# Two tiles centred without their standard deviation, and seven q tiles parked as fp32 copies, in a fused linear-attention and SwiGLU kernel

## The chip, the cores and the metric

One core of one Trainium2 chip. The metric is the device time of the kernel in microseconds (us); lower is better. The engines are TensorE (PE, with its weight loads shown as PEld), VectorE (DVE), ScalarE (ACT), GpSimd (POOL) and SyncE (SP, which here only issues DMAs).

## The reference

The input `x` is 2048 x 512 in bf16. It is normalised once, and both branches read the normalised `xn`:

```python
def _A_ref(x, wqkv, wo):
    H = 32; Dh = D // H                       # D = 512, Dh = 16
    qkv = (x @ wqkv) split into q, k, v by head
    phi = lambda t: jnp.where(t > 0, t + 1, jnp.exp(t)) + 1e-6
    pq, pk = phi(q), phi(k)
    kv = jnp.einsum("bhsd,bhse->bhde", pk, v)
    z = jnp.einsum("bhsd->bhd", pk)
    num = jnp.einsum("bhqd,bhde->bhqe", pq, kv)
    den = jnp.einsum("bhqd,bhd->bhq", pq, z)[..., None] + 1e-6
    return (num / den) @ wo

def _B_ref(x, w_gate, w_up, w_down):          # F = 1792
    return (silu(x @ w_gate) * (x @ w_up)) @ w_down

xn = _layernorm(x)                            # (x - mean) / sqrt(var + 1e-5)
return x + _A_ref(xn, A_wqkv, A_wo) + _B_ref(xn, B_w_gate, B_w_up, B_w_down)
```

## The kernel before

**Order.** The kernel is written as one list of operations for all engines. `K.add` notes for each operation its engine, what it reads and what it writes, and derives the semaphore waits; each engine then runs its own operations strictly in the order of the list. There is no scheduler behind it: the order is written out by hand as a string of steps, `run("S0 R0 S1 L0 ...")`, a letter for the step and a number for the tile of 128 rows. There are 16 tiles.

**Stage 1, the string.** For tile t:
- `S` takes the row statistics on DVE (L228, L231); `R` computes `ln(var + eps)` and then `exp(-0.5 ...)` = 1/std on ACT (L235, L237).
- The tile is normalised to `xn` by one of three steps: `L` on DVE (L241), `N` and `A` on POOL and ACT (L246, L251), or `P` on POOL (L256, L259).
- `xn` is transposed to `xnT`: tiles 0, 1 and 2 on PE (`T`, L269), with the PSUM result copied out by ACT (`E`, L276) or DVE (`V`, L278); the other 13 by a DMA transpose that SP issues (`D`, L284).
- `k` and `q` are the projections (L297), each four matmuls of 512 columns into one PSUM bank. The banks 4 to 7 are used in a ring: a projection takes the bank of the fourth one before it, and waits until that bank's readers are through.
- The feature map is computed in three steps. ACT takes the exp of the bank (`x`, `y`, L305), POOL limits it to 1 (`m`, `n`, L309), and DVE adds `max(bank, 1e-6)` and writes `pk` or `pq` (`s`, `u`, L316).
- `G` accumulates `xn^T pk` over the tiles in the banks 0 to 3 (L321).

Ahead of the string PE runs ten matmuls on a constant, `keep_busy(NWARM, 512)` (L218), and within it two of 256 columns (`F2`).

**Stage 2, the feed-forward loop.** 56 steps `gu(j)` each compute one gate and one up block of 128 x 512 (L384), ACT takes the silu (L392) and DVE multiplies (`hop`, L397) into `hT[C % 2, fc]`. C counts the four chunks of four tiles. In the first steps the sums that the attention branch still needs are put in between: the copies of G (`gt_evac`), the sum of `pk` over the tiles (`z_add`, L334, tiles 0 to 9 on POOL and 10 to 15 on DVE), and the matmul that spreads z. Later steps carry the denominators (`pz_mul`, `divide`). From the second chunk on, `otile` computes the output tiles (L463, L467) and writes them out.

**DMAs.** SP issues the x tiles and half of the qkv weights first, then the transposes `D` in the order of the string, and behind the last of them the weights of stage 2 (`fload`, `dload`); ACT issues three loads at the start.

Of the kernel before, what the change touches and what calls it, by code (L numbers as in the profile page):

```python
# [9 lines left out]
P = 128  # L10
# [10 lines left out]
HPG = P // DH  # L21
NH = D // DH

NWARM = 10
NFILL = 3
O_SLOT = {4: 0, 7: 1, 10: 2, 13: 3}
PZ_AT = {9 + 11 * t // 4: t for t in range(16)}
DIV_AT = {j + 1: t for j, t in PZ_AT.items()}
# [79 lines left out]
def bass_parallel_sum__linear_attn_block__swiglu_ffn__prompt_kernel(nc, A_x, A_wqkv, A_wo, B_x, B_w_gate, B_w_up, B_w_down, out):  # L108
# [5 lines left out]
    with contextlib.ExitStack() as es:  # L114
# [4 lines left out]

        x_sb = sb("x_sb", [P, NT, D], bf)  # L120
        xn = sb("xn", [P, NT, D], bf)
        xnT = sb("xnT", [P, NDC, S], bf)
        wqkv = sb("wqkv", [P, NDC, 3 * D], bf)
        wo = sb("wo", [P, NG, D], bf)
# [24 lines left out]
        lnv = sb("lnv", [P, NT], f32)  # L149
        rstd = sb("rstd", [P, NT], f32)  # L150
        nm = sb("nm", [P, NT], f32)
        banks = [E(nc.psum_tensor("pb%d" % i, [P, 512], f32)) for i in range(8)]

        def B(i):
            return ("bank", i)
# [27 lines left out]


        K.add("act", lambda e: e.preload_act_table_set("natural_log_exp_and_others"))
        for h, eng in ((0, "sp"), (1, "act")):
            load(eng, ("x", 0, h), x_sb[:, 0, h * 256:h * 256 + 256], xin[0:P, h * 256:h * 256 + 256])
        xload("sp", 1)
        wload("act", 1, 0, 2)
        wload("sp", 1, 1, 2)  # L190
        xload("act", 2)
        wload("act", 0, 0, 2)
        xload("sp", 3)
        wload("sp", 0, 1, 2)
        for t in range(4, 16):
            xload("sp", t)

# [24 lines left out]


        def xk(t):
            return [("x", t)] if t else [("x", 0, 0), ("x", 0, 1)]

        def bn1(t):
            K.add("dve", lambda e: e.bn_stats(stats[:, t, :], x_sb[:, t, :]), r=xk(t), w=[("st", t)])  # L228
# [4 lines left out]
        def rs(t):  # L233
            sl = slice(t, t + 1)
            K.add("act", lambda e: e.activation(lnv[:, sl], mv[:, t, 1:2], ACT.Ln, bias=eps5[:, :], scale=1.0),  # L235
                  r=[("mv", t), ("eps5",)], w=[("lnv", t)])
            K.add("act", lambda e: e.activation(rstd[:, sl], lnv[:, sl], ACT.Exp, scale=-0.5),  # L237
                  r=[("lnv", t)], w=[("rs", t)])

        def lna_dve(t):  # L240
            K.add("dve", lambda e: e.tensor_scalar(  # L241
# [24 lines left out]

        def transp(t, b, lo=0, hi=NDC):
            tb = tview(b, hi - lo)
            K.add("pe", [(lambda e, c=c: e.transpose(tb[:, c - lo, :], xn[:, t, c * P:(c + 1) * P], ident[:, :]))  # L269
                         for c in range(lo, hi)], r=[("xn", t), ("ident",)], w=[B(b)])  # L270

        def evac(t, b, eng="act", lo=0, hi=NDC):
            src = tview(b, hi - lo)
            dst = xnT[:, lo:hi, t * P:(t + 1) * P]
            if eng == "act":
                K.add("act", lambda e: e.activation(dst, src, ACT.Copy), r=[B(b)], w=[("xnT", t, lo)])  # L276
            else:
                K.add("dve", lambda e: e.tensor_copy(dst, src), r=[B(b)], w=[("xnT", t, lo)])  # L278

        def xkeys(t):  # L280
            return [("xnT", t, 0), ("xnT", t, 2)] if t == 0 else [("xnT", t, 0)]

        def dmat(t):
            K.add("sp", lambda e: e.dma_start_transpose(out=xnT[:, :, t * P:(t + 1) * P], in_=xn[:, t, :]),  # L284
                  r=[("xn", t)], w=[("xnT", t, 0)], dma=True)


        ring = [0]
# [3 lines left out]
            ring[0] += 1  # L292
            return 4 + (ring[0] - 1) % 4

        def proj(col, i, t):
            b = nextbank()
            K.add("pe", [(lambda e, c=c: e.matmul(  # L297
                banks[b][:, :], xnT[:, c, t * P:(t + 1) * P], wqkv[:, c, col:col + D],
                start=(c == 0), stop=(c == NDC - 1))) for c in range(NDC)],
                r=xkeys(t) + [("wqkv", i, 0), ("wqkv", i, 1)], w=[B(b)])  # L300
            at[i, t] = b

        def phi_exp(i, t):
            b = at[i, t]
            K.add("act", lambda e: e.activation(ef[:, b - 4, :], banks[b][:, :], ACT.Exp), r=[B(b)], w=[("ef", b - 4)])  # L305

        def phi_min(i, t):
            buf, bkey = ef[:, at[i, t] - 4, :], ("ef", at[i, t] - 4)
            K.add("pool", lambda e: e.tensor_scalar(  # L309
                out=buf, in0=buf, scalar1=1.0 + 1e-6, scalar2=0.0, op0=ALU.min, op1=ALU.max),  # L310
                r=[bkey], w=[bkey])

        def phi_sum(i, t):
            b = at[i, t]
            dst, dkey = ((pk[:, t, :], ("pk", t)) if i else (pq[:, t, :], ("pq", t)))
            K.add("dve", lambda e: e.scalar_tensor_tensor(  # L316
                out=dst, in0=banks[b][:, :], scalar=1e-6, in1=ef[:, b - 4, :], op0=ALU.max, op1=ALU.add),
                r=[B(b), ("ef", b - 4)], w=[dkey])

        def gacc(t):  # L320
            K.add("pe", [(lambda e, c=c: e.matmul(  # L321
                banks[c][:, :], xn[:, t, c * P:(c + 1) * P], pk[:, t, :],
                start=(t == 0), stop=(t == NT - 1))) for c in range(NDC)],
                r=[("xn", t), ("pk", t)], w=[B(c) for c in range(NDC)])


        NZP = 10
# [1 line left out]
        def z_add(half, i):  # L329
            acc, key = zacc[:, half, :], ("zacc", half)  # L330
            t = NZP * half + i
            first, fkey = (pk[:, t - 1, :], ("pk", t - 1)) if i == 1 else (acc, key)
            K.add("dve" if half else "pool",
                  lambda e: e.tensor_tensor(out=acc, in0=first, in1=pk[:, t, :], op=ALU.add),  # L334
                  r=[fkey, ("pk", t)], w=[key])

        def stat(t):
            bn1(t)
            bn2(t)

        steps = {
            "S": stat, "R": rs, "L": lna_dve, "P": lna_pool, "N": nmr, "A": lna_act, "T": lambda t: transp(t, t % 4),
            "E": lambda t: evac(t, t % 4), "V": lambda t: evac(t, t % 4, "dve"), "D": dmat,
            "k": lambda t: proj(D, 1, t), "x": lambda t: phi_exp(1, t), "m": lambda t: phi_min(1, t), "s": lambda t: phi_sum(1, t),
            "q": lambda t: proj(0, 0, t), "y": lambda t: phi_exp(0, t), "n": lambda t: phi_min(0, t), "u": lambda t: phi_sum(0, t), "G": gacc,
            "F": lambda t: keep_busy(t, 256)}

        def run(text):
            for w in text.split():
                steps[w[0]](int(w[1:]))  # L350

        run("""
            S0 R0 S1 L0 R1 L1 S2 T0 E0 F2 T1 V1 R2 L2 k0 k1 x0 m0 S3 T2 S4 x1 m1 E2 R4 s0 q1 R3 L4 k2 x2 N3 A3
            q2 s1 m2 y1 S5 R5 G0 D4 S6 s2 n1 G1 q0 y2 G2 D3 u1 R6 q4 N5 A5 S8 y0 k3 n2 N6 A6 u2 k4 y4 x3 n0 x4
            n4 m3 u0 m4 S13 D5 q3 R8 u4 s3 P8 D6 S7 k5 y3 R13 D8 n3 G3 s4 x5 k6 R7 S9 R9 N7 q6 G4 m5 A7 u3 s5
            S12 x6 q5 G5 N9 m6 S10 A9 y6 s6 y5 q8 R10 D7 k8 N13 n6 R12 u6 y8 G6 n5 x8 D9 u5 A13 k7 x7 S15 S11 k9
            P10 n8 u8 x9 R11 m8 D10 s8 m7 q9 m9 R15 P15 s7 y9 q7 G7 k10 D13 n9 L11 L12 s9 y7 q10 D11 G8 y10 n7
            n10 S14 G9 R14 x10 u7 u9 u10 k11 m10 N14 x11 s10 D15 q13 y13 A14 D12 m11 n13 s11 q11 y11 k12 D14 u13
            x12 m12 k13 k15 n11 x15 m15 u11 G10 x13 m13 s12 G11 q15 q14 y15 n15 s13 s15 k14 x14 m14 y14 q12 s14
            G12 y12 n12 n14 u15 G13 G14 u14 u12 G15  # L360
        """)
        fload("sp", "wg", wg, B_w_gate, 0)
        fload("sp", "wu", wu, B_w_up, 0)
# [31 lines left out]
        def hop(j):  # L395
            C, fc = j // NFC, j % NFC
            K.add("dve", lambda e: e.tensor_tensor(  # L397
                out=hT[:, C % 2, fc, :], in0=banks[gb(j) + 1][:, :], in1=sil[:, j % 2, :], op=ALU.mult),
                r=[B(gb(j) + 1), ("sil", j % 2)], w=[("hT", C % 2, fc)])


        def gt_evac(c, eng):
# [34 lines left out]
        def divide(t):  # L437
            i = t % 2
            K.add("dve", lambda e: e.tensor_reduce(  # L439
                out=den[:, i, :], in_=heads(pz[:, i, :]), axis=mybir.AxisListType.X, op=ALU.add),  # L440
                r=[("pz", i)], w=[("den", i)])
            K.add("dve", lambda e: e.tensor_scalar(
                out=den[:, i, :], in0=den[:, i, :], scalar1=1e-6, scalar2=None, op0=ALU.add),
                r=[("den", i)], w=[("den", i)])
            K.add("dve", lambda e: e.reciprocal(rden[:, i, :], den[:, i, :]), r=[("den", i)], w=[("rden", i)])
            K.add("dve", lambda e: e.tensor_tensor(  # L446
                out=heads(pq[:, t, :]), in0=heads(pq[:, t, :]),
                in1=rden[:, i, :][:, :, None].broadcast_to([P, NH, DH]), op=ALU.mult),
                r=[("pq", t), ("rden", i)], w=[("pq", t)])
            K.add("sp", lambda e: e.dma_start_transpose(  # L450
                out=pk[:, t, :].rearrange("p (g s) -> p g s", g=NG), in_=pq[:, t, :]),
                r=[("pq", t)], w=[("pk", t)], dma=True)
# [113 lines left out]
```

## Time and profile before

| | |
|---|---|
| median of 6 runs | 213.4 us (213.19 to 213.69) |
| profiled execution, its own time | 213.16 us |
| its span | 211.5 us |
| granted TensorE clock | 1.00 |
| PE busy | 207.9 us, 98% of the span |
| DVE, ACT, POOL busy | 125.3, 69.8 and 55.6 us |
| first projection matmul starts | 6.54 us |
| first gate matmul starts | 48.48 us |
| issue of the first gate weights | 39.15 us |

The profile shows one execution, recorded by the hardware. Busy time is summed by engine; a matmul's recorded length includes its way through the array, so that matmuls overlap, and a PE that is called busy need not run at its peak. The times within the trace start with the span. Groups of instructions are named by the line of the kernel, the engine, and the tiles written and read.

### The profile page before, as it was taken

The numbers are of one execution on the slowest core, as the hardware profiler recorded it, in microseconds if no ns is written. First come the engines' busy times: TensorE is split into PE (matmuls) and PEld (weight loads), VectorE is DVE, ScalarE is ACT, GpSimd is POOL, SyncE is SP. The second block draws the span as 40 slices with busy tenths as digits, with TensorE's granted clock in tenths as the row PEclk, the third lists the DMA queues.
The fourth block names the chain that finished last, engine by engine and source line by source line (L and its number), as shares of the span: only waits on it lengthen the run. The fifth ranks groups of instructions, "written<-read, shape, count | busy, mean of one in ns | idle before, by whom it ended". The sixth has DMA issues, their size and how long they took to land.

```text
span 211.5 us, 2659 instructions
## 1 busy us (share of the span) xinstructions
PE 207.9 (98%) x991; PEld 95.9 (45%) x991; DVE 125.3 (59%) x217; ACT 69.8 (33%) x138; POOL 55.6 (26%) x81
## 2 busy tenths in 40 slices
PE   7999999999999999999999999999999999999996
PEld 2444444444544444444444444444444444444455
DVE  3899985546874788664654765573649453532121
ACT  3797974546364333122131313021123122130000
POOL 3267665559923222220210220120204000000000
PEclk9999999999999999999999999999999999999999
DMA  5942423499910021103101011101011101100101
GB/s 180 356 114 48 77 58 68 105 382 371 357 52 0 4 49 25 50 0 53 25 25 40 9 29 50 25 25 50 17 35 25 50 16 39 25 25 9 40 25 53
DMA packets 26765, 15.78 MB, mean 75 GB/s; under 512 B 16512, under 2 KB 26752, under 8 KB 26752
## 3 DMA queue, kind: packets, MB, share of 16 engines
q1 hardware_dynamic: 25920, 14.88, 25.3%
q10 hardware_dynamic: 832, 0.72, 1.0%
q8 instruction: 8, 0.13, 0.3%
q14 instruction: 5, 0.04, 0.1%
HBM read 9.70 MB, written 2.10 MB: 56 GB/s over the span
## 4 chain that ended last, share of the span: by engine, by line
PE 96%; DMA 1%; DVE 1%; ACT 1%; SPq 0%; issue 0%
PE pb L384 46%; PE pb L467 23%; PE pb L297 13%; PE pb L463 7%; PE pb L321 7%; DMA x_sb<-in_A_x_dram 1%; PE pb L409 0%; PE pb L457 0%; DVE stats L228 0%; ACT ef L305 0%; ACT xnT L276 0%; DVE out_sb L473 0%; DVE xn L241 0%; SPq L159 0%; PE pb L269 0%
## 5 line engine op out<-in xcount | busy, mean ns | idle before, releaser
L392 ACT ACTIVATE sil<-pb 128x512 bf16<-128x512 f32 x56 | 33.3, 597 | 101.2 <-PE pb L384 98.8
L397 DVE TENSOR_TENSOR hT<-pb,sil 128x512 bf16<-128x512 f32 x56 | 38.0, 687 | 36.2 <-PE pb L384 33.4
L384 PE MATMUL pb<-xnT,wg 128*128 128x512 bf16 x224 | 57.8, 379 | 0.0
L384 PE MATMUL pb<-xnT,wu 128*128 128x512 bf16 x224 | 57.8, 379 | 0.0
L467 PE MATMUL pb<-wd,hT 128*128 128x512 bf16 (+1 forms) x238 | 51.2, 366 | 0.0
L434 POOL TENSOR_TENSOR pz<-pq,zbc 128x512 f32<-128x512 bf16 x16 | 18.6, 1162 | 86.0 <-DVE den L439 78.5
L467 PEld LDWEIGHTS pb<-wd,hT 128*128 128x128 bf16 x238 | 23.3, 98 | 25.1
L384 PEld LDWEIGHTS pb<-xnT,wu 128*128 128x128 bf16 x224 | 21.9, 98 | 26.0
L384 PEld LDWEIGHTS pb<-xnT,wg 128*128 128x128 bf16 x224 | 21.9, 98 | 25.9
L473 DVE TENSOR_TENSOR out_sb<-pb,x_sb 128x512 bf16<-128x512 f32 (+1 forms) x17 | 11.2, 660 | 33.5 <-PE pb L467 33.5
L297 PE MATMUL pb<-wqkv,xnT 128*128 128x512 bf16 x128 | 29.6, 379 | 0.1
L309 POOL TENSOR_SCALAR ef<-ef 128x512 bf16<-128x512 bf16 x32 | 19.4, 612 | 19.1 <-ACT ef L305 18.9
L305 ACT ACTIVATE ef<-pb 128x512 bf16<-128x512 f32 x32 | 18.3, 591 | 9.4 <-PE pb L297 9.3
L297 PEld LDWEIGHTS pb<-wqkv,xnT 128*128 128x128 bf16 x128 | 12.3, 98 | 15.1 <-ACT xnT L276 0.6
L446 DVE TENSOR_TENSOR pq<-pq,rden 128x512 bf16<-128x512 bf16 x16 | 17.5, 1094 | 0.6
L463 PE MATMUL pb<-M,pk 128*128 128x512 bf16 (+1 forms) x68 | 16.6, 366 | 0.0
L321 PE MATMUL pb<-pk,xn 128*128 128x512 bf16 x64 | 15.4, 379 | 0.0
L316 DVE SCALAR_TENSOR_TENSOR pk<-pb,ef 128x512 bf16<-128x512 f32 x16 | 10.8, 679 | 4.9 <-POOL ef L309 4.9
L316 DVE SCALAR_TENSOR_TENSOR pq<-pb,ef 128x512 bf16<-128x512 f32 x16 | 10.7, 682 | 3.9 <-POOL ef L309 3.9
L228 DVE BATCH_NORM_STATS2 stats<-x_sb 128x6 f32<-128x512 bf16 x16 | 10.9, 679 | 3.3 <-DMA x_sb<-in_A_x_dram 3.3
L439 DVE TENSOR_REDUCE den<-pz 128x32 f32<-128x512 f32 x16 | 10.8, 675 | 0.0
L334 POOL TENSOR_TENSOR zacc<-zacc,pk 128x512 f32<-128x512 f32 x8 | 10.3, 1292 | 0.6
(46 smaller groups left out, 76.8 us busy)
## 6 DMA issues: line engine op xcount, KB each, us to landing
out_dram<-out_sb SPq DMA_DIRECT2D x15, 128.0 KB, 1.7
x_sb<-in_A_x_dram SPq DMA_DIRECT2D x14, 128.0 KB, 4.3
wg<-in_B_w_gate_dram SPq DMA_DIRECT2D x2, 896.0 KB, 7.9
wu<-in_B_w_up_dram SPq DMA_DIRECT2D x2, 896.0 KB, 9.9
wd<-in_B_w_down_dram SPq DMA_DIRECT2D x2, 896.0 KB, 13.8
wqkv<-in_A_wqkv_dram ACTq DMA_DIRECT2D x2, 256.0 KB, 4.2
wqkv<-in_A_wqkv_dram SPq DMA_DIRECT2D x2, 256.0 KB, 4.7
wqkv<-in_A_wqkv_dram SPq DMA_DIRECT2D x1, 512.0 KB, 8.0
```

The source lines that it names most:

```text
L297: K.add("pe", [(lambda e, c=c: e.matmul(banks[b][:, :], xnT[:, c, t * P:(t + 1) * P], wqkv[:, c, col:col + D], start=(c == 0), stop=(c == ...
L305: K.add("act", lambda e: e.activation(ef[:, b - 4, :], banks[b][:, :], ACT.Exp), r=[B(b)], w=[("ef", b - 4)])
L309: K.add("pool", lambda e: e.tensor_scalar(out=buf, in0=buf, scalar1=1.0 + 1e-6, scalar2=0.0, op0=ALU.min, op1=ALU.max), r=[bkey], w=[bkey])
L316: K.add("dve", lambda e: e.scalar_tensor_tensor(out=dst, in0=banks[b][:, :], scalar=1e-6, in1=ef[:, b - 4, :], op0=ALU.max, op1=ALU.add), ...
L321: K.add("pe", [(lambda e, c=c: e.matmul(banks[c][:, :], xn[:, t, c * P:(c + 1) * P], pk[:, t, :], start=(t == 0), stop=(t == NT - 1))) for ...
L384: fns.append(lambda e, c=c, b=b, w_=w_: e.matmul(banks[b][:, :], w_[:, c, fc * P:(fc + 1) * P], xnT[:, c, C * 512:(C + 1) * 512], start=(c ...
L392: K.add("act", lambda e: e.activation(sil[:, j % 2, :], banks[gb(j)][:, :], ACT.Silu), r=[B(gb(j))], w=[("sil", j % 2)])
L397: K.add("dve", lambda e: e.tensor_tensor(out=hT[:, C % 2, fc, :], in0=banks[gb(j) + 1][:, :], in1=sil[:, j % 2, :], op=ALU.mult), r=[B(gb( ...
L434: K.add("pool", lambda e: e.tensor_tensor(out=pz[:, t % 2, :], in0=pq[:, t, :], in1=zbc[:, :], op=ALU.mult), r=[("pq", t), ("zbc",)], w=[( ...
L446: K.add("dve", lambda e: e.tensor_tensor(out=heads(pq[:, t, :]), in0=heads(pq[:, t, :]), in1=rden[:, i, :][:, :, None].broadcast_to([P, NH ...
L463: fns = [(lambda e, g=g: e.matmul(banks[bank][:, 0:hi - lo], pk[:, t, g * P:(g + 1) * P], M[:, g, lo:hi], start=(g == 0), stop=False)) for ...
L467: fns = [(lambda e, fc=fc: e.matmul(banks[bank][:, 0:hi - lo], hT[:, C % 2, fc, jj * P:(jj + 1) * P], wd[:, fc, lo:hi], start=False, stop= ...
```

## The change

**Tiles 0 and 1** are only centred: `xc = x - mean`. Tile 0 is centred by DVE in two halves of 256 columns, tile 1 in one piece, with a mean that ACT computes in a pass of its own over x (`M`, an accumulating Copy). Both are transposed by PE, tile 0 in halves into two banks, and projected; the projection is then std times the wanted one. The first half of a tile's projection (`K`, `Q`) and the second (`k`, `q`) are steps of their own. For these tiles the exp has a per-row scale 1/std and bias ln(std), so that the whole feature map comes out std times too large, with limits `cap` and `flo` that are std times the old ones. `G` reads `xg = (x - mean) / std^2` instead of `xn`, z takes `pk` times 1/std, and in the quotient of q the std cancels. ACT gets three more small powers for each of the two tiles (`r`), POOL the limits (`o`) and `xg` (`J`). The normalised `xn` of tiles 0 and 1 is made as well, for stage 2, and comes to `xnT` by two further DMA transposes (15 instead of 13).

**Seven q tiles** (0, 2, 3, 5, 7, 12, 10) are parked: ACT copies the bank to fp32 in SBUF (`z`), writes the exp to `pq`, and DVE forms the sum later from these two. Parked copies, `xc`, `xg` and the transposed `xcT` lie in `hT`, which is not used before stage 2.

**The string** is a new one: statistics, normalisations, projections, feature maps, G steps and transposes all come in another order. The normalising engine changes for several tiles: L241 goes from six tiles to eight, L251 from seven to three, L259 from three to six. `G` runs over the tiles in the order 0, 1, 2, 7 ... 14, 15, 10, the last eleven of them in one row. The warm-up has eight matmuls instead of ten and the two of 256 columns are gone.

```diff
-NWARM = 10
-NFILL = 3
+CENTRED = (0, 1)
+NWARM = 8
...
+        xc = hT[:, 1, 0:2, :]
+        xg = hT[:, 1, 2:4, :]
+        xcT = hT[:, 1, 4:6, :].rearrange("p a b -> p (a b)").rearrange("p (c s) -> p c s", c=NDC)
...
+        tq = [hT[:, 0, 2 * i:2 * i + 2, :].rearrange("p a b -> p (a b)").bitcast(f32) for i in range(NFC // 2)]
...
+        def powers(t):
+            sl = slice(t, t + 1)
+            K.add("act", lambda e: e.activation(std[:, sl], lnv[:, sl], ACT.Exp, scale=0.5), r=[("lnv", t)], w=[("std", t)])
+            K.add("act", lambda e: e.activation(r2[:, sl], lnv[:, sl], ACT.Exp, scale=-1.0), r=[("lnv", t)], w=[("r2", t)])
+            K.add("act", lambda e: e.activation(lstd[:, sl], lnv[:, sl], ACT.Copy, scale=0.5), r=[("lnv", t)], w=[("lstd", t)])
...
+        def neg_mean(t):
+            K.add("act", lambda e: e.activation(
+                junk, x_sb[:, t, :], ACT.Copy, scale=-1.0 / D, accum_out=negm[:, t:t + 1]),
+                r=xk(t), w=[("negm", t), ("junk",)])
+
+        def centre_half(t, h):
+            K.add("dve", lambda e: e.tensor_scalar(
+                out=xc[:, t, h * H:(h + 1) * H], in0=x_sb[:, t, h * H:(h + 1) * H], scalar1=mv[:, t, 0:1], scalar2=None,
+                op0=ALU.subtract), r=xk(t) + [("mv", t)], w=[("xc", t, h)])
...
+        def xg_pool(t):
+            K.add("pool", lambda e: e.tensor_scalar(
+                out=nmg[:, t:t + 1], in0=mv[:, t, 0:1], scalar1=-1.0, scalar2=0.0, op0=ALU.mult, op1=ALU.add),
+                r=[("mv", t)], w=[("nmg", t)])
+            K.add("pool", lambda e: e.tensor_scalar(
+                out=xg[:, t, :], in0=x_sb[:, t, :], scalar1=nmg[:, t:t + 1], scalar2=r2[:, t:t + 1],
+                op0=ALU.add, op1=ALU.mult), r=xk(t) + [("nmg", t), ("r2", t)], w=[("xg", t)])
...
+        def phi_keep(t):
+            b, slot = at[0, t], later[t]
+            K.add("act", lambda e: e.activation(tq[slot], banks[b][:, :], ACT.Copy), r=[B(b)], w=[("tq", slot)])
+
         def phi_exp(i, t):
             b = at[i, t]
-            K.add("act", lambda e: e.activation(ef[:, b - 4, :], banks[b][:, :], ACT.Exp), r=[B(b)], w=[("ef", b - 4)])
+            buf, bkey = ef[:, b - 4, :], ("ef", b - 4)
+            if i == 0 and t in later:
+                buf, bkey = pq[:, t, :], ("pq", t)
+            if t in CENTRED:
+                K.add("act", lambda e: e.activation(buf, banks[b][:, :], ACT.Exp, bias=lstd[:, t:t + 1], scale=rstd[:, t:t + 1]),
+                      r=[B(b), ("rs", t), ("lstd", t)], w=[bkey])
+            else:
+                K.add("act", lambda e: e.activation(buf, banks[b][:, :], ACT.Exp), r=[B(b)], w=[bkey])
...
+            val, mid, keys = banks[b][:, :], ef[:, b - 4, :], [B(b), ("ef", b - 4)]
+            if i == 0 and t in later:
+                val, mid, keys = tq[later[t]], pq[:, t, :], [("tq", later[t]), ("pq", t)]
             K.add("dve", lambda e: e.scalar_tensor_tensor(
-                out=dst, in0=banks[b][:, :], scalar=1e-6, in1=ef[:, b - 4, :], op0=ALU.max, op1=ALU.add),
-                r=[B(b), ("ef", b - 4)], w=[dkey])
+                out=dst, in0=val, scalar=low, in1=mid, op0=ALU.max, op1=ALU.add),
+                r=keys + lkeys, w=[dkey])
...
         run("""
-            S0 R0 S1 L0 R1 L1 S2 T0 E0 F2 T1 V1 R2 L2 k0 k1 x0 m0 S3 T2 S4 x1 m1 E2 R4 s0 q1 R3 L4 k2 x2 N3 A3
-            q2 s1 m2 y1 S5 R5 G0 D4 S6 s2 n1 G1 q0 y2 G2 D3 u1 R6 q4 N5 A5 S8 y0 k3 n2 N6 A6 u2 k4 y4 x3 n0 x4
...
+            S0 M1 b0 a0 d0 c0 R0 C1 S1 e0 P0 W1 h0 K0 r0 w1 k0 R1 o0 S2 K1 J0 x0 k1 S3 R2 m0 Q0 r1 L2 Q1 x1 o1
+            s0 X2 J1 q0 S5 Y2 D0 q1 R3 k2 m1 R5 L3 y0 s1 P5 G0 D3 S7 x2 q2 y1 m2 D5 S9 G1 z0 n1 s2 z2 n0 q3 R7
+            u1 R9 L7 k3 y2 S15 P9 D7 y3 k5 S8 R15 D9 x3 P15 q5 S13 x5 z3 G2 S4 m3 D15 y5 m5 s3 k7 R4 n5 R13 s5
+            q7 x7 P13 S12 z5 q9 L4 m7 D13 R12 y7 q15 n2 s7 z7 n3 D4 k15 y9 L12 S10 y15 n9 k9 R8 D12 n15 u9 x15
+            G3 N8 u15 x9 m15 A8 k13 m9 s15 R10 D8 q4 s9 x13 N10 S11 A10 m13 q12 y4 s13 D10 k4 R11 n4 S6 z12
+            k12 P11 x4 u4 G7 S14 x12 m4 D11 y12 m12 q8 s4 R6 n12 s12 R14 k8 y8 L6 N14 L1 D6 q10 n8 x8 A14 u8
+            m8 q13 z10 n7 s8 D14 k11 y13 u3 y10 n13 q11 D1 x11 u13 q6 m11 y11 s11 n11 k6 y6 u11 n6 k14 x6 n10
+            u6 k10 x14 m6 u12 q14 m14 x10 s6 m10 G9 y14 s14 n14 s10 G4 u10 G5 u7 G11 u5 u2 G13 u14 G8 u0 G12
+            G6 G14 G15 G10
         """)
```

In the string, `d`, `c` and `W`, `X` are transposes on PE (halves of tile 0; tiles 1 and 2), `e`, `h` and `w`, `Y` the copies out of PSUM that belong to them (ACT, except `w` on DVE), `b`, `a` the half centrings and `C` the centring of tile 1 on DVE.

## The prediction

> **What bounds the kernel now.** I read the busy shares first, then the chain that ended last, then the timeline of the first 12 us, last the busy times by stretch. The shares and the chain:
>
> ```profile
> PE 207.9 (98%) x991; PEld 95.9 (45%) x991; DVE 125.3 (59%) x217; ACT 69.8 (33%) x138; POOL 55.6 (26%) x81
> PE 96%; DMA 1%; DVE 1%; ACT 1%; SPq 0%; issue 0%
> ```
>
> TensorE is the chain for 96% of the span. The rest of it is almost all in the head; the chain in order of time (start us, us, what):
>
> ```profile
> 1.26 2.90 DMA x_sb<-in_A_x_dram
> ...
> 5.69 0.42 DVE xn L241
> ...
> 6.16 0.40 PE pb L269 x4
> 6.56 1.89 PE pb L297 x8
> 8.45 0.02 issue
> 8.48 0.60 ACT ef L305
> 9.07 0.50 ACT xnT L276
> 9.57 0.05 issue
> 9.62 1.90 PE pb L297 x8
> 11.52 1.73 PE pb L321 x8
> ```
>
> Load of x, statistics, normalisation, transpose; then projections; then a wait for tile 2's evacuation, queued on ACT behind an exp. From there no gap: in the timeline (start us, busy us, engine, line) the first G step (four L321 matmuls) and the first gate matmul are
>
> ```profile
> 11.35 1.89 PE L321 MATMUL pb<-pk,xn 128*128 128x512 bf16 x8
> 48.48 1.03 PE L384 MATMUL pb<-xnT,wg 128*128 128x512 bf16 x4
> ```
>
> Between them lie 27 projections and 16 G steps, 43 units of four matmuls: 37.13 us, 0.8635 us each, which is the back-to-back rate. So the kernel's time is set by one number, the **head**: start of the gapless stretch less the units done before it. Before: 11.35 - 5 x 0.8635 = 7.03 us. The change can win only by a smaller head, and loses every gap it opens later. The stretch has helpers with little room early on (us of each window; columns: PE, PEld, DVE, ACT, POOL):
>
> ```profile
> 10.00:20.00 10.00, 10.00 (x49) 4.49 (x47) 9.26 (x20) 8.96 (x24) 6.04 (x13) 1.00 0.43 106
> 20.00:30.00 10.00, 10.00 (x48) 4.58 (x47) 8.93 (x20) 8.14 (x21) 6.86 (x14) 1.00 0.35 67
> 30.00:40.00 10.00, 10.00 (x48) 4.52 (x47) 6.05 (x11) 5.58 (x13) 6.00 (x12) 1.00 0.27 53
> ```
>
> **What the Trainium skill says.** "TensorE: Matmul & The Clock Gate", Part 1: the array runs at half clock until a busy window of about 3.4 us has passed. The trace agrees: weight loads of the warm-up are 0.43 us apart up to 4.21, and from 4.25, 3.41 us after the first matmul at 0.84, the array is fast (the two 256-column fillers take 0.38 together). The page also says that the window is free-running; one trace can't show that. "ScalarE: Activation LUTs", What ACT_TABLE_LOAD costs: each per-partition operand adds about 93 ns to an ACTIVATE. Here Ln with one takes 287 ns, Exp without 203; L251 with two 801 against 591 for L305: agrees. "SBUF — State Buffer", Who interferes with whom: the second of a VectorE two-port or two-input operation and a GpSimd one blocks fully. The trace is milder: the DVE adds of L334 take 0.68 alone and 0.89 to 1.04 beside the GpSimd ones, and L241, at 29.89 beside L309, is no longer than its maximum of 415 ns.
>
> **Part 1, the head.** Before, tile 0 waits for mean and rstd, and L241 comes behind tile 1's statistics. Now it is centred with the mean alone. By measured durations:
> - DVE: L228 3.12 to 3.81, L231 to 4.03 as before. Two half centrings: L241 takes 0.40 at 512 columns; by "VectorE: DVE Perf Modes", Mode 4×_2P, four elements a cycle, half the columns saves 0.07, so about 0.32: done 4.39 and 4.64. Bounds 0.25 to 0.40.
> - PE: two transposes of each half, done about 4.7 and 5.0.
> - ACT: the new pass for tile 1's mean starts when x1 lands, 4.16. No such row; 0.6 (L276, same size) to 1.0 with an accumulator; I take 0.7: to 4.88. Behind it queue Ln and Exp of tile 0 (0.33 apart, then 0.11), the half evacuations (0.60 less 256 x 0.83 ns = 0.38): first 5.23 to 5.61, second to 5.90.
> - PE: first half k0 at 5.66 (before: 6.54). Its second half needs the weights issued at 1.73, landing 4.4 later: 6.13, so 6.15 to 6.58. Tile 1: centred by 5.33, transposed by 5.8, copied on DVE behind its statistics by 6.47; k1 6.58 to 7.45, the half q0 and q1 to 8.31.
> - ACT: exp of k0 with two operands, 0.78, from 6.79; Ln and Exp of tile 2 queue behind it, to 8.00. DVE normalises tile 2, 8.06 to 8.46. PE, idle 0.2, transposes it to 8.91; the other halves of q0, q1 run 8.73 to 9.59. ACT evacuates tile 2 behind the exp of k1, to 9.65; k2 starts 9.70.
>
> New head: 9.70 - 4 x 0.8635 = 6.25, **0.78 us less**. The ACT pass at 1.0 makes it 0.55; a pass of 0.6 and quick halves gain 0.9. Two of ten warm-up matmuls and two fillers go; PE waited for DVE there (0.6 at L269), so nothing.
>
> **Part 2, the stretch.** DVE gains two L241, two halves and a centring (about +1.9 us); ACT loses four L251 (-3.2) and gains seven fp32 copies (+4.1, as L305), six small powers (+1.2), the mean pass (+0.7), operands and halves (+0.9); POOL gains three L259 pairs (+3.0), two scaled copies (+2.0), four floors (+0.8) and loses four L246 (-1.1). None fills 38 us. But seven q banks are freed by an ACT copy, not the DVE sum, which moves some 4 us of DVE work behind 30 us and loads ACT: from exp of q0 (10.4) to that of q12 (29.1), nineteen exps and six copies at 0.48 apart, nine Ln/Exp pairs at 0.43, two L251 at 0.71 are 17.7 of 18.7 us, **95%**.
>
> Deadlines, with the bank ring of four and each queue in order: q3 (13.15) needs xnT of tile 3: normalised by 10.5, the DMA transpose 2.5 (2.4 to 3.5 seen), so 13.05, behind the new transpose of tile 0 and x loads that land until 12.4. k3 (14.02) needs q1's sum: 13.98, behind two statistics. q7 (18.33) needs k3's sum: 18.2. q15 (20.06) needs a GpSimd normalisation and a transpose: 19.2 to 20. The rest have 0.2 us or more. I take 0.2 lost, bounds 0 and 1.2 (four gaps of 0.3). A gap doesn't come back.
>
> **Part 3, the end of the stretch.** Five deferred sums run on DVE beside the GpSimd z adds, from 40 us. A sum with two SBUF inputs has no row; 0.68 (L316) to 1.04 (L334 contended): at most 5.2 us, ended by 46, before the GT copies at 47.7. The two extra DMA transposes (1.19 us of SP's queue each) stand ahead of the weight loads. Their last now follows tile 14's at 33.2, so wg is issued at 34.4, not 39.15, lands 7.9 later, and is needed at 47.7. The z adds grow by 1.7 us on POOL but start at 40, not 47.2, and are read at 63.2. Later stages keep their matmuls; the floor of tiles 0 and 1 is a 32-column operation on a DVE that is half idle. All nothing; without those margins POOL's 1.7 us would reach the z matmul.
>
> **Sum.** -0.78 + 0.2 = about -0.6. The profiled execution took 213.16 (span 211.5 plus 1.66 around it): 212.56. It was 0.24 under the median of the six runs, 213.4; against that, 212.8.
>
> **Rivals.** (a) Head won, given back: with ACT at 95%, 3% longer operations are 0.5 us, and one late transpose is up to 1.0. For it: margins of 0.1. Against: the run before had DVE at 93% and no gap. Net -0.4 to +0.4: 213.0 to 213.8, likeliest 213.3. (b) Slower: the clock. The eight warm-ups end at 4.25, exactly when the clock opened in this trace; then the array gets six hundred ns of transposes until 5.66. If the window closes later, it sees an idle array and stays at half clock. Two cold us of projections (5.66 to 7.66) cost 1.0, a whole window more another 1.7; from 1.6 us cold the 0.78 is gone. Net +0.2 to +1.9, likeliest 214.0. For it: ten warm-ups reached 4.9. Against: the opening at 3.41 after the first matmul. (c) The seven copies do nothing: DVE saved, ACT spent, no bank freed sooner; then the head's gain stands alone, 212.6.
>
> **Chances.** Forecast with (c) 0.58, (a) 0.24, (b) 0.12, and 0.06 for gaps over 1.2 us by blocking of DVE and GpSimd. A measurement can tell 0.2% (0.43 us) from no change. Faster 0.58, same 0.22, slower 0.20 (a's upper edge lends 0.02). Range 212.3 (head 0.9 and a little) to 213.9, leaving out the worse half of (b) and the long gaps.
>
> **Right or wrong.** Right: first projection near 5.7, k2 near 9.7, first gate matmul near 47.9, no PE wait over 0.3 between. Wrong: 16 early projection matmuls 0.43 apart (clock); PE waits on ACT copies, DVE sums or xnT transposes adding to over 0.8; ACT's mean pass over 1 us; gate matmuls waiting for GT or wg.

## The result, and the profile after

The changed kernel takes 213.91 us (median of 35 runs) against 213.29 for the kernel before (70 runs beside it): a ratio of 1.0034, 95% interval 1.0026 to 1.0042, so some 0.7 us slower. The forecast was 212.8, range 212.3 to 213.9.

The profiled execution has a span of 212.3 us, 0.8 more than before. The shares and the chain (line numbers are now those of the changed kernel: L389 projection, L438 G, L520 gate and up, L417 limit on POOL, L428 sum on DVE, L326 normalisation on DVE):

```profile
PE 208.6 (98%) x987; PEld 95.3 (45%) x987; DVE 127.4 (60%) x221; ACT 72.1 (34%) x150; POOL 64.1 (30%) x93
PE 92%; DMA 3%; ACT 2%; DVE 1%; issue 1%; POOL 0%; SPq 0%
```

TensorE was 96% of the chain and is 92% now; the rest went mostly to DMA and ACT. The timeline of TensorE shows where the gapless stretch begins and ends:

```profile
10.91 1.03 PE L438 MATMUL pb<-pk,hT 128*128 128x512 bf16 x4
...
49.28 1.03 PE L520 MATMUL pb<-xnT,wg 128*128 128x512 bf16 x4
```

The first G step starts at 10.91, with five projections done: the head is 10.91 - 5 x 0.8635 = 6.59 us, 0.44 less than the 7.03 of before. But from there to the first gate matmul it takes 38.37 us, and the 43 units between need 37.13: 1.24 us are gaps. -0.44 + 1.24 = +0.80, which is what the first gate matmul moved (48.48 to 49.28) and what the span grew. The largest gap stands in the chain in order of time:

```profile
22.90 0.23 DVE pq L428
23.13 3.56 DMA xnT<-xn
26.70 0.14 issue
26.83 2.75 PE pb L389 x12
```

PE waits at 26.83 for a DMA transpose, that of tile 12, which q12 reads: it starts 0.82 us later than the matmul rate would have it. Four gaps of 0.07 to 0.13 us at 11.84, 13.71, 14.68 and 24.29 make up the rest. The helpers have little room on the whole stretch (columns as before: PE, PEld, DVE, ACT, POOL):

```profile
10.00:20.00 10.00, 10.00 (x46) 4.18 (x46) 9.66 (x23) 9.43 (x27) 8.44 (x16) 1.00 0.57 127
20.00:30.00 10.00, 9.34 (x44) 3.97 (x42) 8.96 (x18) 8.89 (x22) 7.39 (x15) 1.00 0.52 69
30.00:40.00 10.00, 10.00 (x49) 4.51 (x47) 8.24 (x13) 8.27 (x19) 8.15 (x15) 1.00 0.52 124
```

DVE, ACT and POOL are all at 74 to 97%, where before only DVE and ACT were at 81 to 93%, and that up to 30 us.

The timeline of the SP queue (start, length of the issue) shows how tile 12 got late. These are the transposes of tiles 13, 4 and 12:

```profile
20.11 1.19 SPq L372 DMA_TRANSPOSE xnT<-xn  x1
21.34 1.75 SPq L372 DMA_TRANSPOSE xnT<-xn  x1
23.13 1.27 SPq L372 DMA_TRANSPOSE xnT<-xn  x1
```

The view of DMA issues, asked for each of the three in turn, has their landing (last column, us from issue): 4.0 for tile 13, 3.2 for tile 4, and for tile 12

```profile
xnT<-xn SPq DMA_TRANSPOSE x1, 3.6
```

Most transposes issue in 1.19 to 1.3 us and land 2.5 us after they begin. Here the issue of the second takes 1.75, and all three land 0.7 to 1.5 us late. Beside them the trace has instruction fetches: DMA packets that bring an engine its next instructions. The view of DMA from 8.9 to 34 us lists them (queue and kind: packets, MB, share of 16 engines):

```profile
...
q14 instruction: 3, 0.02, 0.3%
q8 instruction: 1, 0.02, 0.2%
```

The packet of q8 has 16 KB and takes 1.0 us from 21.67 on, beside tiles 13 and 4. It is over before tile 12's transpose begins; but one of q14's, of 8 KB, starts at 25.10, in the middle of that transfer.

### The profile page after: what moved, and what is told of

The parts are those of the page before. It is cut to its first block, busy times and chain, and to the rows that moved or that the text cites. A ratio compares the mean times of both kernels' runs of the same rounds, so it can differ in the third digit from the quotient of the medians.

```text
span 212.3 us, 2693 instructions
## 1 busy us (share of the span) xinstructions
PE 208.6 (98%) x987; PEld 95.3 (45%) x987; DVE 127.4 (60%) x221; ACT 72.1 (34%) x150; POOL 64.1 (30%) x93
## 4 chain that ended last, share of the span: by engine, by line
PE 92%; DMA 3%; ACT 2%; DVE 1%; issue 1%; POOL 0%; SPq 0%
PE pb L520 46%; PE pb L608 23%; PE pb L389 10%; PE pb L604 7%; PE pb L438 6%; DMA xnT<-xn 2%; DMA x_sb<-in_A_x_dram 1%; ACT ef L410 1%; PE pb L356 0%; ACT hT L399 0%; PE pb L545 0%; PE pb L598 0%; ACT ef L407 0%; POOL ef L417 0%; DVE xn L326 0%
## 5 line engine op out<-in xcount | busy, mean ns | idle before, releaser
L520 PE MATMUL pb<-xnT,wg 128*128 128x512 bf16 x224 | 57.8, 379 | 0.0
L520 PE MATMUL pb<-xnT,wu 128*128 128x512 bf16 x224 | 57.8, 379 | 0.0
L520 PEld LDWEIGHTS pb<-xnT,wu 128*128 128x128 bf16 x224 | 21.9, 98 | 26.0 <-DVE hT L533 0.2
L520 PEld LDWEIGHTS pb<-xnT,wg 128*128 128x128 bf16 x224 | 21.9, 98 | 25.9
L389 PE MATMUL pb<-wqkv,xnT 128*128 128x512 bf16 x112 | 25.4, 379 | 0.7 <-DMA xnT<-xn 0.7
L389 PEld LDWEIGHTS pb<-wqkv,xnT 128*128 128x128 bf16 x112 | 10.5, 98 | 14.9 <-DVE mv L259 1.1
L417 POOL TENSOR_SCALAR ef<-ef 128x512 bf16<-128x512 bf16 x22 | 13.8, 637 | 3.9 <-ACT ef L410 3.3
L410 ACT ACTIVATE ef<-pb 128x512 bf16<-128x512 f32 x22 | 12.8, 594 | 2.4 <-PE pb L389 2.2
L438 PE MATMUL pb<-pk,xn 128*128 128x512 bf16 x56 | 12.7, 379 | 0.0
L428 DVE SCALAR_TENSOR_TENSOR pk<-pb,ef 128x512 bf16<-128x512 f32 x14 | 9.2, 681 | 1.3 <-POOL ef L417 1.2
L604 PEld LDWEIGHTS pb<-M,pk 128*128 128x128 bf16 x68 | 6.7, 98 | 7.4
L461 POOL TENSOR_TENSOR zacc<-zacc,pk 128x512 f32<-128x512 f32 x8 | 9.6, 1195 | 0.6
```

The source lines that it names most:

```text
L389: K.add("pe", [(lambda e, c=c: e.matmul(banks[b][:, :], src[:, c, t * P:(t + 1) * P], wqkv[:, c, col:col + D], start=(c == 0), stop=(c == ...
L410: K.add("act", lambda e: e.activation(buf, banks[b][:, :], ACT.Exp), r=[B(b)], w=[bkey])
L417: K.add("pool", lambda e: e.tensor_scalar(out=buf, in0=buf, scalar1=top, scalar2=0.0, op0=ALU.min, op1=ALU.max), r=[bkey] + tkeys, w=[bkey])
L438: K.add("pe", [(lambda e, c=c: e.matmul(banks[c][:, :], src[:, t, c * P:(c + 1) * P], pk[:, t, :], start=first, stop=last)) for c in range ...
L520: fns.append(lambda e, c=c, b=b, w_=w_: e.matmul(banks[b][:, :], w_[:, c, fc * P:(fc + 1) * P], xnT[:, c, C * 512:(C + 1) * 512], start=(c ...
L604: fns = [(lambda e, g=g: e.matmul(banks[bank][:, 0:hi - lo], pk[:, t, g * P:(g + 1) * P], M[:, g, lo:hi], start=(g == 0), stop=False)) for ...
```

## The experiments

Ratios are to the kernel before on the same chip, with the 95% interval; they are not formed from the two medians (in e8 and e14 these alone would give 1.0005 and 1.0080). The runs went to several chips, so kernels are compared best within a group.

### The late transpose, the warm-up

**e4_after_again**: the changed kernel unchanged.

> The changed kernel once more, for a second trace of the same code on the same chip. If the two losses belong to the code, the clock opens at 6.6 again (0.54 us of cold projections) and PE waits 0.8 us at 26.8 for tile 12's xnT; ratio to the kernel before 1.003. If the clock window is free-running, the opening differs from 6.6. If the instruction fetch at 21.7 us, that falls between the transposes of tiles 13 and 4, is what makes tile 12 late, a trace with the fetch elsewhere has no wait there.

214.0 us, 1.0040 (1.0026 to 1.0054). The second trace has the gap at the same place, at 26.36, of 0.52 us, and a larger one, of 0.61, at 13.76, where q3 starts; with 0.07 at 11.41 that is 1.19 us in all. The clock opened near 5.8 instead of 6.6, and the head was 6.17. The 16 KB fetch came at 20.64 and stretched tile 4's issue to 1.44 only; tile 12's transpose began at 22.64 and still took 3.58 us to land, with a fetch of 8 KB at 24.78.

**e2_swap**: k4 ahead of q12.

```diff
-A10 m13 q12 y4 s13 D10 k4 R11 n4 S6 z12 k12 P11 x4 u4
+A10 m13 k4 y4 s13 D10 q12 R11 n4 S6 x4 k12 P11 z12 u4
```

> The changed kernel with two pairs of steps exchanged in the string: the k projection of tile 4 comes ahead of the q projection of tile 12, and the exp of k4 ahead of the copy of q12. All else is the same. Theory (late transpose): PE's 0.82 us wait at 26.83 for tile 12's xnT is in the path in every run; with 0.86 us of other work put in front of it the wait goes, the first gate matmul moves from 49.28 to about 48.5, and the kernel is 0.7 to 0.8 us faster than the changed one, ratio to the kernel before 1.000. Rival (accident of the profiled execution): the wait is not there in most runs, and the time moves by less than 0.2 us. Rival (next in line): the wait reappears at the next projection that lacks data or a bank, and less than half of it is won.

213.0 us, 0.9992 (0.9981 to 1.0003): 1.0 us faster than the changed kernel beside it. In its timeline TensorE runs through the place:

```profile
23.82 4.63 PE L389 MATMUL pb<-wqkv,xnT 128*128 128x512 bf16 x20
28.28 1.03 PE L438 MATMUL pb<-pk,xn 128*128 128x512 bf16 x4
29.14 9.66 PE L389 MATMUL pb<-wqkv,xnT 128*128 128x512 bf16 x43
38.64 9.66 PE L438 MATMUL pb<-pk,xn 128*128 128x512 bf16 x43
48.14 1.03 PE L520 MATMUL pb<-xnT,wg 128*128 128x512 bf16 x4
```

Of the gap 0.15 us is left, and the first gate matmul comes at 48.14, with gaps of 0.48 us in all. So tile 12's late transpose is in the path in the timed runs too, not only in a trace, and it is as large as the whole loss. **e12_swap_again** is the same kernel on another chip:

> k4 ahead of q12 once more, to stand beside the others on the same chip. Ratio to the kernel before 0.998 to 1.000; in the trace no wait above 0.3 us between k2 and the first gate matmul, unless the q weights land after 8.

213.26 us, 1.0001 (0.9985 to 1.0017). The expectation of no wait above 0.3 failed: its trace has 0.71 us at 13.77 (q3) and 0.42 at 27.23. The first is a wait for tile 3's transpose:

```profile
9.91 0.69 DVE xn L326
10.60 0.03 DVE pk L428
10.63 3.00 DMA xnT<-xn
13.63 0.14 issue
13.77 3.61 PE pb L389 x16
```

The sharp gain over the kernel before that the trace of e2_swap suggests is not there on two chips; what holds is that the exchange takes back the loss.

**e1_warm10**: `NWARM = 10`; **e3_both**: that and the exchange.

> The changed kernel with ten warm-up matmuls instead of eight. Theory (the clock): in the changed kernel's trace the array stays cold up to 6.6 us, because it falls idle at 4.25 before it has opened; the first projections run 0.43 us apart, which loses 0.54 us. With ten it opens near 4.4 as before the change, the first transposes come 0.3 later (4.7 instead of 4.4) but hidden behind ACT's rstd, and the first gate matmul moves from 49.28 to about 48.9: 0.3 to 0.5 us faster than the changed kernel, ratio to the kernel before about 1.001. Rival (free-running window): the opening doesn't follow the number of warm-ups; the trace opens somewhere between 4.4 and 7.7, and the time stays within 0.1 us of the changed kernel.

> Both edits: ten warm-ups, and k4 ahead of q12. If the two losses add, the sum of what the two kernels gain alone: 1.0 to 1.3 us faster than the changed kernel, ratio to the kernel before 0.997 to 0.998. If one of the two does nothing alone, what the other gives. If a gap that was closed opens the next one, less than the sum.

e1: 214.07 us, 1.0044 (1.0029 to 1.0059); e3: 213.12, 1.0001 (0.9987 to 1.0015). The clock opened at 4.1 in both traces, as the theory had it, and yet nothing was won. Part of the reason is in the waits of e1 (between 4 and 30 us, in parts; us in total, times, longest):

```profile
...
PEld pb L389 <- DMA wqkv<-in_A_wqkv_dram: 0.9, 1, 0.9
PE pb L389 <- DMA xnT<-xn: 0.8, 1, 0.8
...
PE pb L389 <- DMA wqkv<-in_A_wqkv_dram: 0.4, 1, 0.4
```

The first q projection now waits for its weights (to 7.75; in e3 to 8.04), which hadn't been waited for in the trace with a cold array. A cold k projection fills the time until they land. In e3 that holds the head at 6.55. In e1 the head is 6.26, 0.33 less than in the trace of the changed kernel, but it is given back at tile 12, whose transpose doesn't land earlier for it: q12 starts at 26.65 (26.83 there), and the gap before it is 0.93 us.

### The instruction fetch

**e9_small_warm**: `keep_busy(4 * NWARM, 128)` in place of `keep_busy(NWARM, 512)`; **e11_swap_small_warm**: that with the exchange.

> The changed kernel with its warm-up cut smaller: 32 matmuls of 128 columns instead of 8 of 512, the same columns and the same time on the array (8 x 0.427 = 3.4 us). It has 48 TensorE instructions more ahead of the string, so that the instruction fetch of 16 KB, which in the traces falls at 20.6 to 21.7 us between the DMA transposes of tiles 13, 4 and 12, comes some 24 matmuls of 0.216 earlier, near 16. Theory (the fetch makes tile 12 late): tile 4's transpose issues in 1.2 us instead of 1.4 to 2.5, tile 12 lands by 25.5 and PE's wait of 0.5 to 0.9 us near 26.5 goes; 0.5 to 0.9 us faster than the changed kernel, ratio 1.000 to 1.001, unless the fetch makes the transposes at 15 to 17 us late and opens a wait at q9 or q15. Rival (the queue makes it late): three transposes one behind the other with 1.2 us of issue each are late without a fetch; the wait stays above 0.5 us, ratio 1.003.

> k4 ahead of q12 together with the small warm-up matmuls. If both edits heal the same wait, no more than k4 ahead of q12 alone (ratio 0.999). If the fetch costs something more (in the trace with k4 ahead of q12 0.15 us were left at 26.56), 0.1 to 0.2 us better: 0.998. If the fetch at 16 us opens a wait there, worse by 0.2 to 0.8.

e9: 213.74 us, 1.0021 (1.0012 to 1.0030); e11: 213.2, 1.0003 (0.9988 to 1.0018). In e9 the 16 KB fetch moved only to 20.34, where it falls on tile 13's transpose (issue 1.93 us), and the gap at 26.72 stayed, 0.94 us: not the test it was meant to be. In e11 it moved to 18.45, and there it tells: tiles 13 and 4 issue in 1.19 and 1.27 us and land in 2.4 and 2.5, there is no gap near 26, but tiles 9 and 15 are late, and PE waits 0.58 us for the former at 20.70. From e11's chain:

```profile
16.09 4.48 DMA xnT<-xn
20.57 0.14 issue
20.70 3.61 PE pb L389 x16
```

The gap went where the fetch went, from tile 12 to tile 9. That 48 more TensorE instructions move it (in e9 the next fetch too, from 49.5 to 43.0) points to TensorE's own fetch.

All seventeen traces of this case together say more. Of 210 transposes issued after 12.6 us, 97 had no fetch packet between issue and landing: all of them issued in 1.19 to 1.28 us and landed in 2.40 to 2.56. Each of the 59 that landed later had a fetch packet, of 16 or of 8 KB. One of 8 KB that starts 1.0 to 2.1 us after the transpose leaves the issue alone, but the landing then takes 3.0 to 3.6 us instead of 2.5; tile 12's transpose has such a packet in the trace of the changed kernel, in e4 and in e9. No run moves the 8 KB fetch, so its part rests on these coincidences, and what in the DMA makes a transpose slow beside a fetch wasn't tried.

### The head

**e5_d0_late**: tile 0's transpose from ahead of tile 3's to ahead of tile 1's (`S5 Y2 D0 q1` to `S5 Y2 q1`, `q11 D1` to `q11 D0 D1`), with the exchange. **e8_x3_late**: in addition the load of x tile 3 behind the q weights, `S3` behind `L2`. **e6_x3_late_warm10**: that with ten warm-ups.

> The kernel with k4 ahead of q12, and in addition the DMA transpose of tile 0 moved from ahead of tile 3's to just ahead of tile 1's, the last ones before the weight loads. Theory (SP's queue is in the path early): tile 3's transpose is held by the issue of tile 0's (1.3 us of SP's queue from 8.9 on); without it the wait at q3, 0.2 to 0.6 us in the traces so far, shrinks by 0.1 to 0.3 us, and the kernel gains that: ratio to the kernel before about 0.998. Rival: q3's wait is for the ACT copy of q0 that frees its bank, or for tile 3's normalisation; then nothing changes, ratio 0.999. The weights of stage 2 are issued 1.2 us later, near 37 instead of 36, with 11 us to spare, which costs nothing in either.

> As the run before the last, with eight warm-ups: k4 ahead of q12, tile 0's transpose late, x tile 3 behind the q weights. If the clock opens late (5 to 6.6 us, as in three of three traces with eight), the head is set by cold projections and the earlier weights gain little: ratio about 0.998, with ten warm-ups about 0.2 us better. If the weights set it whatever the clock does, this one gains as much as that with ten: 0.997.

> All edits so far: k4 ahead of q12, tile 0's transpose late, ten warm-ups; and the load of x tile 3 goes behind the q weights, with its statistics behind the normalisation of tile 2. Theory (the q weights are what the head waits for once the clock is open): in the traces with ten warm-ups the first q projection waited for the weights to 7.75 and 8.04. 128 KB less ahead of them are 0.36 us at 355 GB/s, so it starts near 7.4, k2 at 9.3 to 9.5 instead of 9.7 to 10.0, and the kernel is 0.3 to 0.5 us faster than with k4 ahead of q12 alone: ratio 0.997. Rival (next in line): tile 2's normalisation, which waits for Ln and Exp behind the exp of k0, holds k2 where it was; ratio as e5. Rival (slower): tile 3 is late for q3 by the moved statistics, and the time grows by up to 0.5 us.

e5: 212.96 us, 1.0000 (0.9985 to 1.0016); e8: 213.28, 1.0023 (1.0010 to 1.0035); e6: 213.58, 1.0016 (1.0005 to 1.0026). None gains. In these traces the q weights landed later still: in e5 and e8 the first q projection waits to 9.26 and 9.12. That undoes the head: e5's first G step starts at 12.08. q3's wait is gone in e5's trace, but behind a head that is 1.5 us late, which proves nothing. The three expectations failed; that x tile 3 was in the weights' way is not borne out.

**e10_no_centre**: with the exchange, tiles 0 and 1 normalised by DVE again; **e13_no_centre_warm10**: that with ten warm-ups and the two of 256 columns; **e15_both_again**: e3 once more, beside e13.

```diff
-CENTRED = (0, 1)
+CENTRED = ()
...
-S0 M1 b0 a0 d0 c0 R0 C1 S1 e0 P0 W1 h0 K0 r0 w1 k0 R1 o0 S2 K1 J0 x0 k1 S3 R2 m0 Q0 r1 L2 Q1 x1 o1 s0 X2 J1 q0 S5 Y2 D0 q1 R3 k2
+S0 R0 S1 L0 R1 L1 d0 c0 e0 h0 W1 w1 k0 S2 x0 k1 S3 R2 m0 L2 x1 s0 X2 q0 S5 Y2 q1 R3 k2
```

> The kernel with k4 ahead of q12, and the centring undone: tiles 0 and 1 are normalised by DVE with mean and 1/std as before the change, transposed into the common xnT and projected whole; the mean pass, the three powers, the limits and the scaled copies go, and so do the two further DMA transposes. Parking and the rest of the order stay. Theory (the centring is worth the head): the first projection starts at 6.4 to 6.6 instead of 5.5, k2 near 10.3 instead of 9.7, and the kernel is 0.5 to 0.7 us slower than with k4 ahead of q12 alone: ratio 1.002. Rival (the q weights set the head): they land at 7.2 to 9.2, so an earlier start only waits for them; within 0.2 us, ratio 0.999 to 1.000. Rival (the helpers): ACT and POOL are spared some 4 us of work in the first 12 us, which is worth more than the head; faster.

> k4 ahead of q12 and the centring undone, now with ten warm-up matmuls and the two of 256 columns between the transposes, as before the change. The run without them was 1.1 us slower than with the centring, but its array was cold up to 9.4. Theory (the clock was most of it): it opens near 4.4, k2 starts near 9.6 to 9.9, and the kernel is 0 to 0.4 us slower than the centred one with ten warm-ups: ratio 1.000 to 1.002. Rival (the centring is worth it all): it stays at 1.004 to 1.005.

> k4 ahead of q12 with ten warm-ups once more, to stand beside the run without the centring on the same chip: ratio 0.999 to 1.001; the clock opens near 4.0 to 4.4, and the first q projection waits for its weights to 7.5 to 8.

e10: 214.36 us, 1.0052 (1.0031 to 1.0073), against 1.0001 for e12 beside it. e13: 214.21, 1.0052 (1.0038 to 1.0066), against 213.23 and 1.0006 (0.9993 to 1.0019) for e15, whose first q projection waited for its weights to 8.50. Both kernels without the centring are slower than forecast. So in this order undoing the centring costs 1.0 to 1.1 us, with eight warm-ups and with ten. Not all of it need be the centring's: this isn't quite the head of the kernel before, where `L2` comes ahead of `S3`; here it comes behind, and e13's PE waits 0.7 us for it at 9.36.

**e14_before_warm8**: the kernel before with `NWARM = 8` and without `F2`.

> The kernel before, with eight warm-up matmuls and without the two of 256 columns; nothing else. Theory (fewer warm-ups keep the array cold): the array opens at 6 to 9 us instead of 4.4, up to twelve projection matmuls run 0.43 us apart, and it is 0.5 to 1.5 us slower: ratio 1.003 to 1.007. Rival (the clock's window doesn't follow the warm-up): ratio 1.000.

214.88 us, 1.0062 (1.0039 to 1.0085), its runs from 213.35 to 215.22; the profiled one was the slowest. Its trace shows a cold array (a clock that is not yet open) up to about 9.7; the same eight projections that took 1.90 us before take

```profile
5.30 1.32 PE L269 MATMUL pb<-ident,xn 128*128 128x128 bf16 x8 [0.88 <-DVE xn L241]
6.59 3.40 PE L297 MATMUL pb<-wqkv,xnT 128*128 128x512 bf16 x8
```

3.40 us. In the old order the two warm-ups and the fillers were worth 1.3 us by the ratio; the forecast had called their removal free.

### The parking

**e7_no_park**: with the exchange, no fp32 copies; exp, limit and sum of the seven q tiles where the copy stood (`z0 ... n0 ... u0` becomes `n0 u0` at the place of `z0`, and so on).

> The kernel with k4 ahead of q12, without the parking: for the seven tiles the fp32 copy goes, and exp, limit and sum of q are made where the copy stood, straight from the bank. The order is otherwise the same. Theory (parking is what lets this order run): DVE and POOL have to finish the sum before the bank is free, on a stretch where DVE is 90% busy; the waits at k3, q3 and the projections of 15 to 26 us grow by 0.1 to 0.5 us each, and the kernel is 0.5 to 2 us slower, ratio 1.002 to 1.008. Rival (parking does nothing): ACT, the fullest engine, is spared seven copies of 0.6 us; time within 0.2 us or faster, ratio 0.998 to 1.000.

220.39 us, 1.0338 (1.0313 to 1.0362): beyond what either theory expected, and 7.4 us above e5, which has the parking and ran on the same chip. Ten gaps of 0.3 to 1.5 us between 15 and 42 us, almost all for a bank whose sum is not done (waits between 8 and 60 us, in parts: us in total, times, longest):

```profile
...
PEld pb L389 <- DVE pq L428: 6.5, 6, 1.7
DVE pq L428 <- POOL ef L417: 5.6, 8, 1.4
...
PEld pb L389 <- DVE pk L428: 4.2, 4, 1.8
PE pb L389 <- DVE pq L428: 3.7, 6, 1.2
```

The parking does what it is meant to do; this order can't do without it.

## Why the prediction was wrong

**The stretch, forecast +0.2 us with bounds 0 and 1.2: this is the term that failed.** It was 1.24 in the profiled run and 1.19 in e4. Two of its deadlines were mis-sized.

The first is q12. It stood among "the rest have 0.2 us or more". By the prediction's own head its turn comes six units behind q15's 20.06, at 25.24; tile 12's transpose landed at 26.70 in the profiled run and at 26.22 in e4. It lost 0.82 and 0.52 us, and the exchange shows that this wait is worth the whole loss. Two delays meet there. SP's queue held tile 12 behind tile 4, whose issue stretched from 1.27 to 1.75, and the landing took 3.56 instead of 2.5. An estimate from these figures: without the stretched issue tile 12 would have begun at 22.65, as in e4, and with a landing of 2.5 it would have been there at 25.15, 0.9 before q12's turn at 26.02. The long issue alone would have cost nothing, the long landing alone 0.3. The normalisations of tiles 4 and 12 ended at 20.80 and 21.99, before SP's queue was free for them (21.30 and 23.09).

The second is q3, a deadline that I had called tight. Its data was to land at 13.05; it landed at 13.57 in the profiled run, 13.63 in e4 and e12, and 13.27 in e2. In all four tile 3's normalisation took 0.70 us beside GpSimd instead of 0.40, and in e4 and e12 the landing took 2.9 and 3.0 us; what made these two late stays open. q3 lost 0.13 us behind the slow head of the profiled run, and 0.61 and 0.71 behind the faster ones of e4 and e12. In the profiled run k3 lost 0.12, q7 and q15 nothing.

I had seen landings up to 3.5 and named them, but set them against the tight deadlines only, not against three transposes one behind the other. The landing of 3.5 in the trace before (at 19.94) has a 16 KB fetch in it, at 19.99: the cause stood in the trace that I had.

**The head, forecast -0.78 us: right by mechanism, and by size where the weights are in time.** The steps stand. The mean pass took 0.63 us and 0.19 to read the accumulator, 0.73 from 4.01 to the result (forecast 0.7); the two half centrings 0.28 each (0.32), the half evacuations 0.38 each (0.38); the first projection started at 5.58 (5.66). Tile 2's normalisation came at 8.41 (8.06), since x0's exp waited for cold k projections to 7.18 (6.79). In four traces with the changed head and eight warm-ups of 512 columns, the head is 6.59 (profiled), 6.17 (e4), 6.21 (e2) and 6.07 (e12), 6.26 on average: the forecast 6.25. That the average comes so near is partly luck; the spread was left out. The array opened at 6.6 here, and in traces with a trimmed warm-up anywhere from 3.8 (e5) to about 9.7 (e14). I had read 4.25 from the trace before, where eight warm-ups end; the last two of its ten start 0.30 us apart, between the cold 0.43 and the fast 0.22, which puts the opening near 4.4, behind the end of eight.

And the prediction took the q weights' landing, 7.05, for a fixed number, with 0.4 us to spare. They land at 7.1 to 9.2 in the traces, and where they are late the head's gain is gone. The kernel before reads them at 8.50.

A smaller head also has to get past q3. The start of q3 less the eight units before it is 6.80 us in the profiled run, 6.85 in e4, 6.86 in e12 and 6.49 in e2, against 7.03 before: of 0.78 us, 0.2 are left in three of them and 0.5 in e2. With all gaps up to the first gate matmul, head and gaps of the exchanged kernel add up to 6.69 in e2 and 7.36 in e12. So both late weights and the wait at q3 stand between it and the forecast gain; which of them holds the timed runs back is not shown by an experiment.

**The helpers' loads**: DVE +2.1 us (forecast +1.9), ACT +2.3 (+3.7), POOL +8.5 (+6.4). DVE's agreement is luck: L326 normalises seven tiles, one more than before and not two as counted, but the seven take 3.8 us where six took 2.4. ACT's 95% was a slip, too: the terms given for it make 17.3 us, 92%.

**The shared port** was read wrongly: the prediction found the trace milder than a full block. It is a full block. Four normalisations on DVE begin in the profiled run while GpSimd works on a tile of 128x512; they take 0.48, 0.70, 0.74 and 0.67 us, and each ends 0.14 to 0.15 us after the GpSimd operation does. In all traces together 33 such normalisations began 0.3 us or more before the end of the GpSimd operation, and all 33 ended 0.143 to 0.148 us after it. The L241 at 29.89 that I took for the rule began 0.22 us before GpSimd was through and ended 0.18 after: too little was left of the block to show.

**Rivals.** (a), head won and given back, is what happened, by its own mechanism of a late transpose, priced there at up to 1.0; but its total of +0.4 at most was too small, since it kept the full head. (b), the clock, was in play with 0.3 us of head in the profiled run, and its price showed in e14 on the old order; but more warm-ups bring nothing here (e1, e3), because tile 12 and the weights are next. (c), parking without effect, fell with e7.

**The end of the stretch** went as worked out: the sums of parked tiles ran 0.67 to 1.09 us (0.68 to 1.04), no matmul waited for G's copies or the gate weights.

## What to carry to other kernels

Where one engine runs without a gap, a change of order is priced by the worst landing seen, not the median, at every deadline; a chain of transfers in one queue adds its lateness up. When a trace has one transfer that is slower than its like, look for what ran beside it before calling it spread. An earlier start is worth only the distance to the next arrival: look up when the data of the second step lands, and of the steps after it, before counting the gain of the first. However an order was found, look in the trace for its single largest wait; here exchanging two pairs of steps took back the whole loss.

## What the runs showed of the hardware

- Instruction fetches go with late DMA transposes on the same core. Of the transposes issued after 12.6 us, those that meet no fetch issue in 1.19 to 1.28 us and land 2.40 to 2.56 us after their start (97 in 17 traces). With a fetch of 16 KB, by its place TensorE's, they issue in up to 2.5 and land in up to 4.3 us, with one of 8 KB in its midst in 3.0 to 3.6, with both in up to 4.6. The wait moved with the 16 KB fetch (e11).
- A normalisation on DVE (128x512, bf16, SBUF to SBUF) that begins while GpSimd works on such a tile ends 0.14 to 0.15 us after GpSimd does, and takes up to 0.74 us in the profiled run instead of 0.40.
- The clock's opening isn't fixed by the code: near 6.6 and 5.8 us in two traces of the changed kernel; at 3.9 to 6.8 us in traces with ten warm-up matmuls, at 3.8 to 9.7 with eight.
- An accumulating ACTIVATE is followed by a read of the accumulator, 0.19 us of its own.
- The q weights issued at 2.26 us landed between 7.1 and 9.2 in traces of one and the same order of loads.
